# A fetch of list entries waits for the scatters of its own batch's units only

## The chip, the cores and the metric

The kernel runs on one core of one Trainium2 chip. The metric is the device time of one execution in microseconds (us), from a median over repeated runs. One core has five engines with instruction streams of their own: PE (TensorE, matrix products; PEld is its loading of weights), DVE (VectorE), ACT (ScalarE), POOL (GpSimd) and SP (SyncE, which here only reads registers and issues transfers). Engines wait for each other, and for transfers, on semaphores. Sixteen DMA engines carry the transfers of the core. An instruction that waits holds up what stands behind it in the stream of its own engine; this goes for the issue of a transfer too.

## The reference, cut to what matters

```
# gated linear attention, 4 batches x 8 heads x 768 steps x 48
for t in range(S):
    state = alpha[:, :, t, :, None] * state + einsum('bhd,bhe->bhde', k[:, :, t], v[:, :, t])
    y[:, :, t] = einsum('bhd,bhde->bhe', q[:, :, t], state)
x = y.transpose(0, 2, 1, 3).reshape(3072, 384)
# noisy top-2 router over 8 experts, each 384 -> 1024 -> 384
noisy = x @ w_gate + log1p(exp(x @ w_noise)) * noise
top2 = the two largest of noisy;  top2_w = softmax over them
for e in range(8):
    for k in range(2):
        mask = top2[:, k] == e
        h = maximum(x[mask] @ w1[e], 0)
        out[mask] += top2_w[mask, k, None] * (h @ w2[e])
```

All is float32. Each of the 3072 tokens is worked on by two experts, so there are 6144 pairs of token and expert.

## The kernel before, in words

**Attention.** The 3072 tokens are 24 chunks of 128, n = 0 to 23. The chunk of number n is loaded by four transfers on SP's queue (`load_values` L162, `load_chunk` L158: tiles `vt`, `a_in`, `k_in`, `q_in`, 192 KB each), two chunks at a time in buffers. A chunk's results go to the DRAM tensor `x_rows`, and its router decides two experts for each token.

**Lists.** Three chunks make a unit, u = 0 to 7. When a unit is routed, `give` (with `enter`, L585) ranks its 768 pairs within their experts and scatters one entry per pair (token, weight, expert, rank; 16 bytes) into the DRAM tensor `table`, where each expert has a region of its own. That is six indirect DMAs of 128 rows each, issued by POOL one after another (`put_entries`, L136). It happens at the end of chunk 3u+4.

**Tiles and batches.** The experts' work is cut into tiles of 128 entries of one expert. After each unit `plan_tiles` decides how many tiles the entries so far fill, and hands out a batch of them: `GIVEN = [0, 5, 11, 17, 23, 29, 35, 55]` gives where each unit's batch ends, so tiles 0 to 4 are given out after unit 1, 5 to 10 after unit 2, and so on to 29 to 34 after unit 6; the rest, up to 50 in the plain case, after unit 7. `plan` holds each tile's expert and first row in `table`. A batch of unit u is worked on beside chunks 3u+8 to 3u+10, so the work for one batch lies over the routing of later units.

**One tile.** It needs its 128 entries (`load_tab`, L687: a transfer `tab<-table` on SP's queue), the first-layer weights of its expert (`load_w1`, L695: `w<-in_moe_w_dram`, 1.5 MB, also on SP's queue, two buffers), its rows of x (`gather_x`, L719, an indirect DMA by POOL) and their transposes (`turn_x`, L728 on PE, L730 on DVE). `layer1` is L739 on PE with the ReLU by ACT at L741, in two halves; `layer2` is L751, with its scaling by ACT at L768. `get_half` (L758) fetches the other half of an output row; `combine` scatters by L769 and L776.

**Order.** The whole program is one order, written out by hand (L864 to L920). Pieces of a chunk and steps of tiles take turns; each engine works through its own instructions in that order. The tile numbered i has four steps, of which the first loads the weights for tile i+1 and gathers the rows for tile i+2. The first four fetches of a batch are issued together, two chunks ahead of the batch (L906). The later ones, the fifth and sixth, are put ahead of the first step of the tile four places earlier (L831):

```
if i + 4 < min(GIVEN[u], ALWAYS):
    steps[0] = lambda go=steps[0]: (load_tab(i + 4), go())
```

So on SP's queue the fetch for tile i+4 stands directly ahead of the weights for tile i+1. Each fetch is made to wait for all scatters into `table` that stand ahead of it in the order (`take_tile`, L144). When the first of the late fetches of a batch comes, the next unit's six scatters already stand ahead of it.

The list `entries` has the clearing of the table first, and then the scatters in order, 6 a unit.

Of the kernel before, what the change touches and what calls it, by code (L numbers as in the profile page):

```python
# [9 lines left out]
F32 = mybir.dt.float32  # L10
# [4 lines left out]
AFTER = mybir.DependencyInfo(mybir.DependencyClass.Sync, mybir.DependencyReason.DATA)  # L15
# [3 lines left out]
def kernel(  # L19
# [28 lines left out]
    nc = tc.nc  # L48
# [3 lines left out]
    C = 128  # L52
# [7 lines left out]
    UT = UC * C  # L60
    NU = NT // UC
# [13 lines left out]
    def pool(name, bufs, on=ctx, **kw):  # L75
        return on.enter_context(tc.tile_pool(name=name, bufs=bufs, **kw))
# [45 lines left out]
    table = dram.tile([TROWS, 4], U32, name="table")  # L122


    entries, taken = [], []

    def clear_table(on):
# [13 lines left out]
        tc.add_manual_dep(put.ins, entries[0].name, AFTER, reason="the table is cleared first")  # L141
        entries.append(put.ins)

    def take_tile(get):  # L144
        for put in entries:
            tc.add_manual_dep(get.ins, put.name, AFTER, reason="reads any row of the table")
        taken.append(get.ins)

    NIN = 2
# [526 lines left out]
    def experts(on):  # L676
# [7 lines left out]
        tabs, w1s, xts, os_, wheres = {}, {}, {}, {}, {}  # L684
        to_half, from_half, to_out = [], [], []

        def load_tab(i):  # L687
            if i >= NTILE:
                return
            r = nc.values_load(plan[0:1, i, 1:2], engines=[mybir.EngineType.SP], min_val=0, max_val=TROWS - C,  # L690
                               skip_runtime_bounds_check_because=WHY)
            tabs[i] = on["tab"].tile([C, 4], F32, name="tab")
            take_tile(nc.sync.dma_start(out=tabs[i], in_=table.bitcast(F32)[ds(r, C), :]))

        def load_w1(i):  # L695
            if i >= NTILE:
# [88 lines left out]
    def tile_steps(i, do, units):  # L785
        load_tab, load_w1, gather_x, turn_x, layer1, layer2, get_half, combine = do

        def first():
            if i + 1 < units[1]:
                load_w1(i + 1)  # L790
            if i + 2 < units[1]:
                gather_x(i + 2, units[0])
            layer1(i, 0)

        def second():
            layer1(i, 1)

        def third():
            if i + 1 < units[1]:
                turn_x(i + 1)  # L800
            get_half(i, units[0])
            layer2(i, 0)

        def fourth():
            layer2(i, 1)
            combine(i, units[0])

        return [first, second, third, fourth]

    def pools(es, name):  # L810
        on = {"one": pool(name + "one", 1, es), "two": pool(name + "two", 2, es), "three": pool(name + "three", 3, es),
              "tab": pool(name + "tab", 10, es)}
        for x, bufs in (("h", 2), ("o", 1), ("tp", 2), ("sc", 1), ("y", 1)):
            on[x] = pool(name + "ps_" + x, bufs, es, space=PS)
        return on


    with ExitStack() as es:
        on = pools(es, "")
        (load, load_v, alphas, keys, queries, scores, masked, turn_k, state, output, turn_y, route,  # L820
         choose_part, give, out_of_range) = fast_gla(on)
        do = experts(on)
        load_tab, load_w1, gather_x, turn_x = do[:4]
        starts = [0] + GIVEN[:-1]
        unit_of = [u for u in range(NU) for _ in range(starts[u], GIVEN[u])]

        def steps_of(i):
            u = unit_of[i]
            steps = tile_steps(i, do, (u + 1, min(GIVEN[u], ALWAYS)))
            if i + 4 < min(GIVEN[u], ALWAYS):  # L830
                steps[0] = lambda go=steps[0]: (load_tab(i + 4), go())  # L831
            return steps


        def last_tiles(i):
            if i == NTILE:
                return
            number = nc.values_load(tiles_i[0:1, 0:1], min_val=0, max_val=NTILE,
                                    skip_runtime_bounds_check_because="a count of tiles")
            with tc.If(number > i):  # L840
                load_tab(i)
                load_w1(i)
                gather_x(i, NU)
                turn_x(i)
                for step in tile_steps(i, do, (NU, i + 1)):
                    step()
                last_tiles(i + 1)


        LAG = 8  # L850
        held = []
        W2_AT = [0, 3, 6, 9, 12, 15, 18, 21, 24, 28, 32]
        beside = []
        for n in range(NT + 2 * UC):
            u, part = divmod(n - LAG, UC)
            beside.append([])
            if 0 <= u < NU - 1 and GIVEN[u] > starts[u]:
                each = -(-(GIVEN[u] - starts[u]) // UC)
                beside[n] = list(range(starts[u] + each * part, min(starts[u] + each * (part + 1), GIVEN[u])))
        while not beside[-1]:  # L860
            beside.pop()
        beside.append(list(range(starts[NU - 1], ALWAYS)))

        with tc.manual_schedule():  # L864
            load(0)
            load(1)
            load_v(0)
            for n in range(2):
                alphas(n)
                keys(n)  # L870
                queries(n)
                load(n + 2) if n == 0 else load_v(1)
            scores(0)
            masked(0)
            turn_k(0)
            for n, tiles in enumerate(beside):
                work = [step for i in tiles for step in steps_of(i)]
                chunk = [lambda: (load_v(n + 2), load(n + 3), state(n)), lambda: alphas(n + 2), lambda: keys(n + 2),
                         lambda: scores(n + 1), lambda: (queries(n + 2), masked(n + 1)),
                         lambda: (choose_part(n - 2, 1), route(n - 1)), lambda: turn_k(n + 1), lambda: output(n),  # L880
                         lambda: turn_y(n - 1)]
                last = [lambda: (choose_part(n - 1, 0), give(n - 2))]
                if n == 0:
                    last.append(lambda: held.append(load_router(on)))
                if n == 1:
                    last.append(lambda: clear_table(on["two"]))
                if n == 2:
                    chunk.insert(1, lambda: turn_noise(held.pop(), on))
                w2_parts = [lambda i=i: load_w2(i) for i in range(W2_AT[n], W2_AT[n + 1])] if n < len(W2_AT) - 1 else []

                if n < LAG:
                    last += w2_parts
                else:
                    chunk[0:0] = w2_parts
                if n == NT + 1:
                    chunk.insert(0, lambda: out_of_range(0))
                    last.append(lambda: out_of_range(1))

                for ahead in (2, 1):
                    nxt = beside[n + ahead] if n + ahead < len(beside) else []  # L900
                    if not nxt or nxt[0] not in starts:
                        continue
                    lo, u = nxt[0], unit_of[nxt[0]]
                    some = range(lo, min(lo + 4, GIVEN[u]))
                    if ahead == 2:
                        last.append(lambda some=some: [load_tab(i) for i in some])  # L906
                    else:
                        chunk.insert(3, lambda: (load_w1(lo), [gather_x(i, u + 1) for i in some[:2]]))
                        chunk.append(lambda: turn_x(lo))
                chunk += last  # L910
                done = 0
                for j in range(len(work)):
                    work[j]()
                    upto_j = len(chunk) * (j + 1) // len(work)
                    for piece in chunk[done:upto_j]:
                        piece()
                    done = upto_j
                for piece in chunk[done:]:
                    piece()
            last_tiles(ALWAYS)  # L920
    redo = nc.values_load(again_i[0:1, 0:1], min_val=0, max_val=2 * C,
                          skip_runtime_bounds_check_because="a count of at most 2 C rows")
    with tc.If(redo > 0):
        taken.clear()
        with ExitStack() as es:
            on = pool("g_clear", 1, es)
            clear_table(on)
        with ExitStack() as es:
            general_gla(es)
        with ExitStack() as es:  # L930
            do = experts(pools(es, "g_"))
            for i in range(4):
                do[0](i)
            do[1](0)
            for i in range(2):
                do[2](i, NU)
            do[3](0)
            for i in range(NTILE):
                do[0](i + 4)
                for step in tile_steps(i, do, (NU, NTILE)):  # L940
                    step()

# [29 lines left out]
```

## Time and profile before

| | |
|---|---|
| runs | median of 3: 877.54 us (875.82 to 878.76) |
| the profiled execution | 869.29 us, its span from first to last instruction 867.6 us |
| mean granted clock of PE in it | 0.944 of full speed |
| busy | PE 779.7 us (90%), POOL 339.1 (39%), DVE 274.5 (32%), ACT 198.8 (23%) |
| DMA | 146.59 MB moved, mean 169 GB/s |

The profile is one execution on the chip. Busy time is summed per engine over its span; idle time of an engine is put down to the last event that released it (an instruction of another engine, a DMA, "issue" where nothing is seen, "remote" where the event's origin isn't resolved). A row of the timeline is the start, the duration, the engine (SPq is SP's queue), the line of the kernel, the operation and what it writes and reads, and in square brackets how long the engine was idle before it and what ended that.

### The profile page before, as it was taken

What the parts mean: (1) busy time and instruction counts of PE and PEld (TensorE: products, weight loads), DVE (VectorE), ACT (ScalarE), POOL (GpSimd) and SP (SyncE); (2) the same over time, 40 slices, a digit from 0 to 9 for tenths busy, and PEclk for the clock granted to TensorE, in tenths of its full rate; (3) what the DMA queues carried; (4) which work ended last, traced back from release to release, by engine and by line L of the source; (5) the groups of instructions that cost most, each with busy time, mean ns of one, the idle gap of its engine ahead of it and who ended that gap; (6) DMA issues with size and microseconds to landing.
All of it is one profiled execution on the core that took longest, in us unless ns stands there. A gap on an engine that the chain in (4) does not pass through costs nothing. (4 is left out here: it accounts for less than half of the span.)

```text
span 867.6 us, 14567 instructions
## 1 busy us (share of the span) xinstructions
PE 779.7 (90%) x5249; PEld 636.5 (73%) x5249; DVE 274.5 (32%) x968; ACT 198.8 (23%) x383; POOL 339.1 (39%) x436
## 2 busy tenths in 40 slices
PE   7888788899899997999899995999599999999992
PEld 5777677688678775888678784787487788888881
DVE  7565755334433334125333241124111111111110
ACT  3343440224122321223122220122111111111110
POOL 4235435343625235334524344245333333333331
PEclk9898877999989999999989998999799999999997
DMA  9898784955295715974184515551555445555530
GB/s 175 190 271 212 216 181 140 270 172 141 57 276 161 223 61 126 256 201 135 35 277 142 195 67 176 186 192 53 177 183 199 163 167 175 190 193 195 201 115 13
DMA packets 158888, 146.59 MB, mean 169 GB/s; under 512 B 117612, under 2 KB 133698, under 8 KB 158804
## 3 DMA queue, kind: packets, MB, share of 16 engines
q1 hardware_dynamic: 136288, 111.79, 44.8%
q0 software_dynamic: 14592, 23.75, 9.4%
q10 hardware_dynamic: 7924, 9.97, 3.4%
q8 instruction: 47, 0.77, 0.4%
q14 instruction: 37, 0.30, 0.1%
HBM read 131.95 MB, written 30.00 MB: 187 GB/s over the span
## 5 line engine op out<-in xcount | busy, mean ns | idle before, releaser
L739 PE MATMUL h_ps<-xt,w 128*128 128x128 f32 x2448 | 293.3, 279 | 17.6 <-DMA w<-in_moe_w_dram 16.1
L739 PEld LDWEIGHTS h_ps<-xt,w 128*128 128x128 f32 x2448 | 286.8, 195 | 26.5 <-issue 16.8
L751 PE MATMUL o_ps<-w,h 128*128 x816 | 284.7, 498 | 3.6 <-issue 2.5
L751 PEld LDWEIGHTS o_ps<-w,h 128*128 128x128 f32 x816 | 152.7, 195 | 99.0 <-issue 11.7
L769 POOL DMA_INDIRECT half_rows<-o,where x51 | 61.2, 1200 | 303.5 <-ACT o L768 257.0
L741 ACT ACTIVATE h<-h_ps 128x512 f32<-128x512 f32 x102 | 60.9, 597 | 308.1 <-PE h_ps L739 168.6
L775 DVE TENSOR_TENSOR prev<-prev,o 128x384 f32<-128x384 f32 x51 | 28.5, 559 | 258.0 <-ACT o L768 233.6
L730 DVE COPY xt<-x_ps 128x384 f32<-128x384 f32 x51 | 28.1, 552 | 176.1 <-PE x_ps L728 164.8
L768 ACT ACTIVATE o<-o_ps,tab 128x384 f32<-128x384 f32 x51 | 29.6, 581 | 188.5 <-PE o_ps L751 188.5
L758 POOL DMA_INDIRECT prev<-half_rows,where x51 | 53.7, 1052 | 28.0 <-DMA half_rows<-o,where 13.6
L719 POOL DMA_INDIRECT x_in<-x_rows,where x51 | 53.5, 1049 | 24.1 <-issue 11.7
L776 POOL DMA_INDIRECT out_dram<-prev,where x51 | 51.1, 1002 | 17.9 <-issue 12.7
L136 POOL DMA_INDIRECT table<-entry,place_u x48 | 48.8, 1017 | 15.0 <-issue 12.2
L291 POOL TENSOR_TENSOR k_P<-k_P,over 128x512 f32<-128x512 f32 x24 | 28.3, 1180 | 65.5 <-DVE over L281 50.9
L275 DVE TENSOR_TENSOR_SCAN P_all<-a_all,least 128x516 f32<-128x516 f32 x24 | 30.7, 1280 | 55.3 <-ACT a_all L271 45.4
L345 POOL TENSOR_TENSOR S<-S,end 128x384 f32<-128x384 f32 x20 | 20.1, 1006 | 50.2 <-DVE S L343 49.4
L196 PE MATMUL y<-q_P,S 128*128 128x128 f32 x192 | 31.2, 315 | 3.7 <-ACT lgs L221 3.7
L263 PE MATMUL tp<-ident,k_in 128*128 128x128 f32 x96 | 17.7, 316 | 17.5 <-ACT tp L272 12.4
L314 PEld LDWEIGHTS sc<-q_P,k_P 48*128 48x128 f32 x384 | 26.1, 207 | 9.8 <-issue 6.6
L314 PE MATMUL sc<-q_P,k_P 48*128 48x128 f32 x384 | 31.0, 307 | 2.4 <-POOL k_P L291 2.4
L196 PEld LDWEIGHTS y<-q_P,S 128*128 128x128 f32 x192 | 28.6, 226 | 5.7 <-ACT lgs L221 4.3
L319 DVE COPY_PREDICATED MT<-upto,sc 128x512 f32<-128x512 uint32 x48 | 31.9, 718 | 0.0
(144 smaller groups left out, 667.5 us busy)
## 6 DMA issues: line engine op xcount, KB each, us to landing
w<-in_moe_w_dram SPq DMA_DIRECT2D x51, 1536.0 KB
w<-in_moe_w_dram SPq DMA_DIRECT2D x32, 384.0 KB
a_in<-in_alpha_dram SPq DMA_DIRECT2D x24, 192.0 KB
k_in<-in_k_dram SPq DMA_DIRECT2D x24, 192.0 KB
q_in<-in_q_dram SPq DMA_DIRECT2D x24, 192.0 KB
vt<-in_v_dram SPq DMA_DIRECT2D x24, 192.0 KB
x_rows<-y_sb ACTq DMA_DIRECT2D x24, 192.0 KB
half_rows<-y_sb ACTq DMA_DIRECT2D x24, 192.0 KB
```

The costliest lines, as they stand in the source:

```text
L136: put = nc.gpsimd.indirect_dma_start(out=table, out_offset=bass.IndirectOffsetOnAxis(ap=place, axis=0), in_=entry, in_offset=None, bounds_ ...
L196: nc.tensor.matmul(y[:, j, :], S_old[:, j].rearrange("p i d -> p (i d)"), q[:, j, :], start=j == 0, stop=False, skip_group_check=True)
L275: nc.vector.tensor_tensor_scan(P_all[:, 0:NP * CB], a_all[:, 0:NP * CB], least.rearrange("p j t -> p (j t)"), 0.0, op0=ALU.mult, op1=ALU.max)
L314: nc.tensor.matmul(c["sc"][i][:, j, :], c["k"][r, j, :], c["q"][r, j, :], start=True, stop=True)
L319: nc.vector.copy_predicated(MTs[n % 2][:, i], mask_upto, sc)
L719: nc.gpsimd.indirect_dma_start(out=x_in[i % NB], out_offset=None, in_=x_rows[0:units * UT, :], in_offset=bass.IndirectOffsetOnAxis(ap=wher ...
L739: nc.tensor.matmul(h_ps[:, fo, :], w1[:, a, ds((part * FO // 2 + fo) * C, C)], xt[:, a, :], start=a == 0, stop=a == KO - 1)
L741: nc.scalar.activation(os_[i]["h"][part], h_ps, AF.Relu)
L751: nc.tensor.matmul(o["ps"], o["h"][part][:, f, :], w2[:, ds(o["e"], 1), fo, :].rearrange("p o d -> p (o d)"), start=fo == 0, stop=fo == FO ...
L758: get = nc.gpsimd.indirect_dma_start(out=prev[i % 2], out_offset=None, in_=half_rows[0:units * UT, :], in_offset=bass.IndirectOffsetOnAxis ...
L769: put = nc.gpsimd.indirect_dma_start(out=half_rows[0:units * UT, :], out_offset=bass.IndirectOffsetOnAxis(ap=where[:, 1:2], axis=0), in_=o ...
L776: put = nc.gpsimd.indirect_dma_start(out=out, out_offset=bass.IndirectOffsetOnAxis(ap=where[:, 2:3], axis=0), in_=prev[i % 2], in_offset=N ...
```

## The change

`take_tile` is told how many units the batch of the tile was given out from. It keeps the waits for the clearing and for the scatters of these units (`2 * UT // C` = 6 a unit), and declares that there is no dependence on the later scatters. `load_tab` gets the number of units as an argument: `u + 1` for the batches in the hand-written order, `NU` = 8 (all units) for the tiles behind number 50 and for the general path that is entered only when a region overflows.

```diff
-    def take_tile(get):
-        for put in entries:
-            tc.add_manual_dep(get.ins, put.name, AFTER, reason="reads any row of the table")
+    def take_tile(get, units):
+        count = 1 + 2 * UT // C * units
+        for put in entries[:count]:
+            tc.add_manual_dep(get.ins, put.name, AFTER, reason="reads any row of the table that these fill")
+        for put in entries[count:]:
+            tc.declare_no_dep(get.ins, put, reason="rows behind those of the tile")
         taken.append(get.ins)
...
-        def load_tab(i):
+        def load_tab(i, units):
             if i >= NTILE:
                 return
...
-            take_tile(nc.sync.dma_start(out=tabs[i], in_=table.bitcast(F32)[ds(r, C), :]))
+            take_tile(nc.sync.dma_start(out=tabs[i], in_=table.bitcast(F32)[ds(r, C), :]), units)
...
-                steps[0] = lambda go=steps[0]: (load_tab(i + 4), go())
+                steps[0] = lambda go=steps[0]: (load_tab(i + 4, u + 1), go())
...
-                load_tab(i)
+                load_tab(i, NU)
...
-                        last.append(lambda some=some: [load_tab(i) for i in some])
+                        last.append(lambda some=some, u=u: [load_tab(i, u + 1) for i in some])
...
-                do[0](i)
+                do[0](i, NU)
...
-                do[0](i + 4)
+                do[0](i + 4, NU)
```

No instruction is added, removed or put elsewhere on any engine; lines behind the new ones move by four. What changes is what some fetches wait for. In the rows below a line is an instruction with its line, operation, what it writes and reads, and the semaphores that it waits for: DMASW are those of indirect DMAs issued by POOL, DMAHW those of other transfers, and DVE_, Activation_ and PE_ those of the engines (DVE, ACT, PE).

The first place is SP's queue in the batch of tiles 23 to 28, where the fetch for tile 27 (the first `tab` row) stands between the weights of tile 23 (`w_4702`) and those of tile 24 (`w_4932`). Before:

```order
L701 DMA w_4702<-in_moe_w_dram 128x3x1024 [waits DMAHW2_49,PE_49]
L690 TENSOR_LOAD plan
L693 ISA
L693 DMA tab<-table 128x4 [waits DMASW5_49,DMASW4_49,DMASW6_49,DMASW3_49,DMASW7_49,DMASW2_49,DMAHW5_49,DVE_49,Activation_49]
L698 TENSOR_LOAD plan
L701 ISA
L701 DMA w_4932<-in_moe_w_dram 128x3x1024 [waits DMAHW7_49,DMAHW6_49,PE_49]
L690 TENSOR_LOAD plan
L693 ISA
L693 DMA tab<-table 128x4 [waits Activation_49]
```

And after the change, the same place:

```order
L705 DMA w_4702<-in_moe_w_dram 128x3x1024 [waits DMAHW2_49,PE_49]
L694 TENSOR_LOAD plan
L697 ISA
L697 DMA tab<-table 128x4 [waits DMAHW3_49,DVE_49,Activation_49]
L702 TENSOR_LOAD plan
L705 ISA
L705 DMA w_4932<-in_moe_w_dram 128x3x1024 [waits DMAHW7_49,DMAHW4_49,PE_49]
L694 TENSOR_LOAD plan
L697 ISA
L697 DMA tab<-table 128x4 [waits DMAHW5_49,DMAHW1_49,Activation_49]
```

The fetch for tile 27 no longer waits for six semaphores of scatters, which were those of unit 6; the weights for tile 24 stand directly behind it as before. The DMAHW numbers, which are given out in turn, fall differently in a few rows: the weights for tile 24 wait on number 4 in place of 6, and the fetch for tile 28 (the last row) on two numbers more. The same goes for the first late fetch of each of the six batches that have one (tiles 4, 9, 15, 21, 27 and 33).

The second place is again SP's queue, earlier: the first of the four fetches issued together ahead of that batch (tile 23, the first `tab` row). Before:

```order
L701 DMA w_4492<-in_moe_w_dram 128x3x1024 [waits DMAHW5_49,DMAHW2_49,PE_49]
L690 TENSOR_LOAD plan [waits DVE_49]
L693 ISA
L693 DMA tab<-table 128x4 [waits DMAHW3_49,DVE_49,Activation_49]
L690 TENSOR_LOAD plan
L693 ISA
L693 DMA tab<-table 128x4 [waits DMAHW4_49,Activation_49]
```

After the change:

```order
L705 DMA w_4492<-in_moe_w_dram 128x3x1024 [waits DMAHW5_49,DMAHW2_49,PE_49]
L694 TENSOR_LOAD plan [waits DVE_49]
L697 ISA
L697 DMA tab<-table 128x4 [waits DMASW5_49,DMASW4_49,DMASW6_49,DMASW1_49,DMASW7_49,DMASW0_49,DMAHW3_49,DVE_49,Activation_49]
L694 TENSOR_LOAD plan
L697 ISA
L697 DMA tab<-table 128x4 [waits DMAHW4_49,Activation_49]
```

The six waits for scatters that the fetch of tile 21 had in the batch before (those for unit 5) stand at this fetch now. In all, seven fetches wait for scatters before, and seven after.

## Rows read from the trace of the kernel before

**Rows 1.** The page's first part: span, and PE's busy time and instructions.

```profile
span 867.6 us, 14567 instructions
PE 779.7 (90%) x5249; PEld 636.5 (73%) x5249; DVE 274.5 (32%) x968; ACT 198.8 (23%) x383; POOL 339.1 (39%) x436
```

**Rows 2.** Waits of PE: who waited for whom, us in all, times, longest us.

```profile
PE h_ps L739 <- DMA w<-in_moe_w_dram: 16.1, 3, 8.9
PE tp L263 <- ACT tp L272: 16.0, 7, 4.8
```

**Rows 3.** Waits of SP's queue, in the same columns.

```profile
SPq L693 <- DMA table<-entry,place_u: 129.1, 7, 37.6
```

**Rows 4.** Timeline of SP's queue, pieces of three stretches between 104 and 640 us.

```profile
105.29 3.09 SPq L158 DMA_DIRECT2D k_in<-in_k_dram  x1
...
153.75 0.00 SPq L693 DMA_DIRECT2D tab<-table  x1
...
492.95 0.38 SPq L701 DMA_DIRECT2D w<-in_moe_w_dram  x1
528.19 0.71 SPq L693 DMA_DIRECT2D tab<-table  x1
529.09 0.37 SPq L701 DMA_DIRECT2D w<-in_moe_w_dram  x1
...
558.38 3.32 SPq L693 DMA_DIRECT2D tab<-table  x4
...
612.77 0.37 SPq L701 DMA_DIRECT2D w<-in_moe_w_dram  x1
```

**Rows 5.** Timeline of PE in the batch of tiles 23 to 28, and at 156 us.

```profile
155.69 0.66 PE L263 MATMUL tp<-ident,k_in 128*128 128x128 f32 x4 [2.80 <-ACT tp L272]
...
503.03 2.92 PE L739 MATMUL h_ps<-xt,w 128*128 128x128 f32 x24
...
526.77 2.85 PE L751 MATMUL o_ps<-w,h 128*128 x8 [2.52 <-issue]
536.01 4.32 PE L739 MATMUL h_ps<-xt,w 128*128 128x128 f32 x24 [6.39 <-DMA w<-in_moe_w_dram]
```

**Rows 6.** Timeline of PE in the batch of tiles 29 to 34.

```profile
585.64 5.52 PE L739 MATMUL h_ps<-xt,w 128*128 128x128 f32 x48
...
608.56 2.85 PE L751 MATMUL o_ps<-w,h 128*128 x8 [1.12 <-ACT h L741]
620.32 7.49 PE L739 MATMUL h_ps<-xt,w 128*128 128x128 f32 x48 [8.91 <-DMA w<-in_moe_w_dram]
```

**Rows 7.** Timeline of DVE, the copies that take xt out of PSUM.

```profile
527.56 0.56 DVE L730 COPY xt<-x_ps 128x384 f32<-128x384 f32 x1 [6.16 <-remote]
...
610.69 0.56 DVE L730 COPY xt<-x_ps 128x384 f32<-128x384 f32 x1 [5.14 <-remote]
```

**Rows 8.** Timeline of POOL, scatters of unit 1 and the first and last of unit 6.

```profile
106.41 1.51 POOL L136 DMA_INDIRECT table<-entry,place_u  x1 [0.30 <-issue]
...
517.58 1.01 POOL L136 DMA_INDIRECT table<-entry,place_u  x1 [0.16 <-POOL entry L596]
...
524.01 0.97 POOL L136 DMA_INDIRECT table<-entry,place_u  x1 [0.31 <-issue]
```

**Rows 9.** Timeline of ACT, where it goes on during the scatters of units 1 and 6.

```profile
109.93 0.17 ACT L221 COPY lgs<-lg 128x16 f32<-128x16 f32 x1 [5.86 <-remote]
...
526.12 0.60 ACT L741 ACTIVATE h<-h_ps 128x512 f32<-128x512 f32 x1 [6.83 <-remote]
```

**Rows 10.** Windows: stretch, length, busy time of each engine (count), PEclk, DMA share, GB/s.

```profile
104.00:110.00 6.00, 1.95 (x16) 1.48 (x14) 5.76 (x16) 0.14 (x3) 5.07 (x5) 0.91 0.87 145
...
506.00:517.00 11.00, 9.85 (x64) 7.22 (x63) 2.85 (x13) 2.24 (x4) 2.15 (x2) 1.00 0.10 36
517.00:531.00 14.00, 10.10 (x58) 7.28 (x57) 4.52 (x28) 1.78 (x3) 9.39 (x13) 1.00 0.20 44
...
614.00:650.00 36.00, 29.68 (x187) 25.34 (x188) 4.45 (x23) 4.15 (x7) 11.50 (x12) 0.86 0.58 208
```

## The prediction

> **What bounds the kernel now.** I read the page's first part, then the waits of PE, the waits of SP's queue, and last the timelines of both at the places where they meet. PE is busy 779.7 of 867.6 us, 90% [rows 1], so its stream sets the end, and a change is worth what it takes out of that stream's gaps. Two causes top the list of its gaps: 16.1 us in three waits for a tile's first-layer weights, and 16.0 us in seven waits for the factor `tp` that ACT writes [rows 2]. SP's queue in its turn waited 129.1 us for scatters into `table`, at seven fetches, up to 37.6 us at one [rows 3]. That sum looks like the prize, and it is not: SP computes nothing, and its waiting costs only where something that stands behind the fetch is late for PE.
>
> It is late in two batches of the six. SP's queue issued a load of weights at 492.95 us, then nothing until 528.19, when the fetch for tile 27 went, and 0.9 us behind it, at 529.09, the weights for tile 24 [rows 4]. PE was done with the tile ahead at 526.77 + 2.85 = 529.62, and idled 6.39 us until it began tile 24 at 536.01 [rows 5]. The same in the next batch: the weights for tile 30 were issued at 612.77 [rows 4], PE was through at 608.56 + 2.85 = 611.41, and began at 620.32, 8.91 us later [rows 6]. The third wait is what is left: 16.1 - 6.39 - 8.91 = 0.8 us. In the other batches the fetch is held as long, but the weights behind it come in time, since beside chunks of attention PE has other work between two tiles.
>
> **What the change removes.** The first late fetch of each of six batches loses its wait for the unit routed meanwhile. The weights behind it are then free to go as soon as their buffer is. For tile 24 this buffer is the one that tile 22 read last; its second half ran from 503.03 for 2.92 us, to 505.95 [rows 5]. From issue to PE's start the weights took 536.01 - 529.09 = 6.9 us [rows 4, 5] and for tile 30 620.32 - 612.77 = 7.6 us [rows 4, 6]. So the weights of tile 24 are there by some 506 + 7 = 513 us, 16 us before PE is ready for them. For tile 30 the buffer comes free when tile 28 is through, 585.64 + 5.52 = 591.16 [rows 6]; the weights are there by 599, 12 us early. Both waits go whole, and the third, 0.8 us long, too: 16.1 us.
>
> *What is late next* at these two places decides whether the whole of it comes back. Tile 24 needs its transposed rows as well. DVE copied them out at 527.56 for 0.56 us, ending at 528.12, and for tile 30 at 610.69, ending at 611.25 [rows 7]. PE is through at 529.62 and 611.41: both copies are in time, the second by 0.16 us only. No gap is left behind.
>
> *The clock.* After both gaps PE's products take longer for a while: the 24 after the first 4.32 us where 24 took 2.92 before [rows 5], 1.4 us more; the 48 after the second 7.49 against 5.52 [rows 6], 2.0 us more. The granted clock was 1.00 up to 531 us and 0.86 in the 36 us from 614 [rows 10], so it fell in the gaps. [...] The gaps of 2.52 and 1.12 us shortly ahead [rows 5, 6] stay; were the clock to fall for these alone, the 3.4 would stay lost. In the stretch with the first of these it did not.
>
> **What it adds.** The first fetch of the next batch now has the waits for scatters. For tile 29, say, that is the first of four fetches issued from 558.38 us [rows 4]. The last scatter of unit 6 ended on POOL at 524.01 + 0.97 = 524.98 [rows 8], and the fetch that waited for its landing went at 528.19 [rows 4], 3.2 us later. So this wait is over 30 us before the instruction comes, and there are seven fetches with such waits as before. The waits on numbers of other transfers that fall anew (the two more at the fetch for tile 28) are for fetches of earlier tiles, issued a batch or more before. I take 0. The bound above is those 3.2 us at each of six fetches, were one to come while the scatters land; 19 us on a queue that has tens of us to spare ahead of a batch.
>
> **The sum.** 16.1 + 3.4 = 19.5 us. From the profiled execution's 869.29 us that gives 849.8. This execution lies 8.25 us (0.9%) under the median of the runs, 877.54, and outside their range; on the scale of the median the forecast is 877.54 - 19.5 = 858.0 us, 2.2% faster. A time within 0.3% (2.6 us) of the median is about what a measurement here can't tell from no change.
>
> **The rivals.**
>
> *More comes back.* At the scatters of each unit, ACT and DVE go on late: at 526.12 after 6.83 us in which nothing that the profile resolves released it, DVE at 527.56 after 6.16 [rows 7, 9]. PE's waits for `tp` are the trace of that on its side (2.80 us at 155.69 [rows 5], the others up to 4.8), and with them the 2.52 us and the 1.12. In all 16.0 + 2.5 + 1.1 = 19.6 us [rows 2, 5, 6]. These gaps lie in the very stretches in which SP is held by a fetch: SP went on at 153.75 [rows 4], 1.9 us before PE did. If SP's held wait causes them, they go, and the time is 858 - 19.6 = 838 us. Against it: during the scatters of unit 1 SP was not held, it issued chunk loads (at 105.29 [rows 4], beside a scatter at 106.41 [rows 8]), and ACT went on just as late, after 5.86 us [rows 9]. What is common to all is POOL issuing six scatters back to back (517.58 to 524.98 [rows 8]), and that stays. Chance 0.08.
>
> *Half comes back.* The next late thing takes one of the two places: the copy for tile 30 has 0.16 us in hand [rows 6, 7], and earlier traffic can move it. Then only the other place is won: 6.4 + 1.4 = 7.8 or 8.9 + 2.0 = 10.9 us, some 868 us. Chance 0.13.
>
> *Nothing comes back.* Another thing holds SP in the same stretch, such as the weights' buffer or a semaphore shared with a late transfer, and the weights come as late as before: 877.5. In the order only the waits named stand there, and the last of them, for the buffer, is over at 506 us. Chance 0.07.
>
> *Slower.* The weights, and in the early batches the chunk loads behind them, now move while POOL scatters. Before, the DMA engines were nearly empty then: a share of 0.20 in the scatters of unit 6 [rows 10], with SP held. If the scatters take longer for the company, the late goings-on of ACT and DVE grow, and PE's gaps with them, at each of six units. The price is at most the time of one load of weights, 7.6 us each, 46 us in all; it decides from 19.5 / 6 = 3.3 us a unit. In the extreme the time would be 877.5 - 19.5 + 46 = 904. Against it: the weights for tile 24 would move in 506 to 517 us, where the share was 0.10 [rows 10], and be there before the first scatter at 517.58 [rows 8]; and with a share of 0.87 at the scatters of unit 1, ACT's idling was 5.86 us, no longer than the 6.83 us at 0.20 [rows 9, 10]. A scatter did take 1.51 us there against 0.97 [rows 8], so a fraction of a us a unit is to be expected, inside the range. Chance 0.06.
>
> [...]
>
> **How the numbers follow.** Forecast 0.66, own range 851 to 865 (the clock's 3.4 us won or not, a us or two a unit lost to the company, and as much for the change of clock from run to run). More 0.08, half 0.13, nothing 0.07, slower 0.06. The range of 8 in 10 reaches over the half case on one side and into the first rival's on the other: 842 to 870 us. Faster 0.66 + 0.08 + 0.13 = 0.87, same 0.07, slower 0.06.
>
> **What would show it.** In the profile of the changed kernel PE's waits for weights should be gone from the list, or under 1 us. SP's waits for the table should fall from 129.1 us to a few. The weights for tile 24 and tile 30 should be issued at about 23 and 21 us before PE begins that tile, and the 24 and 48 products should take 2.9 and 5.5 us. PE's waits for `tp` should be as long as before, 16 us within 3. If those have gone, the first rival is right; if they have grown beyond 35 us, the last one. I'd be wrong above all if PE's 6.39 and 8.91 us come back under another name at the same place, xt or h.

## The result and the profile after

The changed kernel took 819.73 us (median of 4 runs, 812.12 to 822.61) where before took 876.68 us (4 runs, 868.33 to 878.76) beside it: a ratio of 0.9354, 95% interval 0.9266 to 0.9441. That is 57 us, about three times the 19.5 us of the forecast, and below its range. The profiled execution took 819.84 us, its span 818.1.

The waits of PE after the change, the longest three groups (who waited for whom, us in all, times, longest):

```profile
PE tp L267 <- DMA a_in<-in_alpha_dram: 9.7, 3, 5.2
PE total L627 <- DVE picked L595: 5.8, 7, 1.2
PE tp L267 <- ACT tp L276: 3.9, 4, 1.7
```

The wait for weights of [rows 2] is gone, as forecast. But the wait for ACT's `tp` has gone from 16.0 to 3.9 us as well, which I had said would stay. On SP's queue no fetch waits for scatters any more, where [rows 3] had 129.1 us; its timeline at the places of [rows 4] is:

```profile
479.54 0.37 SPq L705 DMA_DIRECT2D w<-in_moe_w_dram  x1
480.48 0.35 SPq L697 DMA_DIRECT2D tab<-table  x1
...
554.33 0.37 SPq L705 DMA_DIRECT2D w<-in_moe_w_dram  x1
```

These are the weights for tiles 24 and 30. PE begins those tiles at 500.23 and 572.99, with nothing to wait for and at a granted clock of 1.00:

```profile
500.23 2.84 PE L743 MATMUL h_ps<-xt,w 128*128 128x128 f32 x24
...
567.83 5.33 PE L755 MATMUL o_ps<-w,h 128*128 x16
572.99 5.52 PE L743 MATMUL h_ps<-xt,w 128*128 128x128 f32 x48
```

The weights are issued 20.7 and 18.7 us ahead, and the 24 and 48 products take 2.84 and 5.52 us where [rows 5, 6] had 4.32 and 7.49. The gaps of 2.52 and 1.12 us ahead of the second half of `o_ps` [rows 5, 6] are gone too: all 16 products run in one piece. ACT tells why. In the scatters of unit 6, where it idled 6.83 us [rows 9], it now goes on as soon as PE is through, the second time 0.04 us after PE's products ended at 489.30 + 5.60 = 494.90:

```profile
492.26 0.60 ACT L745 ACTIVATE h<-h_ps 128x512 f32<-128x512 f32 x1 [4.43 <-PE h_ps L743]
494.94 0.60 ACT L745 ACTIVATE h<-h_ps 128x512 f32<-128x512 f32 x1 [2.08 <-PE h_ps L743]
```

I call what is gone the lags: in six units, while POOL issues its six scatters, ACT had gone on 3.4 to 6.1 us after PE's last product for it, and in the last two of them DVE's copy of xt 5.9 and 5.8 us after. (The expectations below speak of 3 to 9 us; 9.05 us is ACT's longest idle time before it goes on, of which 6.1 us lie behind PE's product.) Laid over each other, product by product, the two profiles part in steps at the six batches that have a late fetch, 48 us in all by the last product. At first sight that is my first rival, the one in which the held fetch makes the lags. The experiments say otherwise.

### The profile page after: what moved, and what is told of

It reads as the page before. It is cut to its first block, busy times and chain, and to the rows that moved or that the text cites. A ratio compares the mean times of both kernels' runs of the same rounds, so it can differ in the third digit from the quotient of the medians.

```text
span 818.1 us, 14568 instructions
## 1 busy us (share of the span) xinstructions
PE 768.1 (94%) x5249; PEld 630.7 (77%) x5249; DVE 273.6 (33%) x968; ACT 198.8 (24%) x383; POOL 339.5 (41%) x436
## 5 line engine op out<-in xcount | busy, mean ns | idle before, releaser
L743 PE MATMUL h_ps<-xt,w 128*128 128x128 f32 x2448 | 289.3, 277 | 1.4 <-DVE xt L734 1.4
L743 PEld LDWEIGHTS h_ps<-xt,w 128*128 128x128 f32 x2448 | 283.4, 193 | 9.2 <-DVE xt L734 1.6
L755 PE MATMUL o_ps<-w,h 128*128 x816 | 277.1, 488 | 0.0
L755 PEld LDWEIGHTS o_ps<-w,h 128*128 128x128 f32 x816 | 149.2, 190 | 91.5 <-issue 2.3
L137 POOL DMA_INDIRECT table<-entry,place_u x48 | 51.0, 1063 | 15.0 <-issue 10.7
L318 PEld LDWEIGHTS sc<-q_P,k_P 48*128 48x128 f32 x384 | 26.1, 207 | 10.5 <-issue 5.9
L285 DVE TENSOR_TENSOR_SCAN over<-a_all,P_all 128x515 f32<-128x515 f32 x24 | 30.2, 1259 | 0.8
```

The costliest lines, as they stand in the source:

```text
L137: put = nc.gpsimd.indirect_dma_start(out=table, out_offset=bass.IndirectOffsetOnAxis(ap=place, axis=0), in_=entry, in_offset=None, bounds_ ...
L318: nc.tensor.matmul(c["sc"][i][:, j, :], c["k"][r, j, :], c["q"][r, j, :], start=True, stop=True)
L743: nc.tensor.matmul(h_ps[:, fo, :], w1[:, a, ds((part * FO // 2 + fo) * C, C)], xt[:, a, :], start=a == 0, stop=a == KO - 1)
L755: nc.tensor.matmul(o["ps"], o["h"][part][:, f, :], w2[:, ds(o["e"], 1), fo, :].rearrange("p o d -> p (o d)"), start=fo == 0, stop=fo == FO ...
```

## The experiments

Kernels that are told together ran on one chip, with before beside them. Not all ran on the same chip, and this turned out to matter, so they are told by chip. Each chip was used at one time only, so a chip and its state at that time can't be told apart; I say chip for both. The letters H, P and so on are names of theories, which the expectations explain.

**First chip (lags): four kernels.** The first is before, unchanged.

> The kernel before, unchanged, once more. In the profile of before ACT and DVE go on 3 to 9 us late after PE's last product at all scatters of units 2 to 7, 2.8 us late at those of unit 1, and about 1 us late in the last tiles (694 to 826 us), where no fetch is held; after the change all of these lags are gone. Theory H (a fetch held on SP's queue makes the lags): here the six lags of 3 to 9 us are there again. Theory P (the lags belong to this execution or to the loaded program as a whole, not to the held fetch): if to the execution, they may be gone and the time about 835 to 850 us; if to the program, they are there again, those of 1 us in the last tiles too.

876.06 us in one run. The lags are there: ACT's wait with no resolved releaser is 46.4 us in 6 times, after 43.5 in the first profile.

The second keeps all waits and changes the order on SP's queue:

```diff
-                steps[0] = lambda go=steps[0]: (load_tab(i + 4), go())
+                steps[0] = lambda go=steps[0]: (go(), load_tab(i + 4))
```

> All waits of before are kept; only the late fetch stands behind the weights of the next tile on SP's queue and no longer ahead of them. It leaves the fetch held as long as before. My forecast's two terms (16.1 us of waits for weights and 3.4 us of slow products) should come back alone: about 858 us, with the six lags still there under theory H. Theory P: the lags are there or gone whatever SP does; if gone, about 830 us, with SP's queue still waiting some 100 us for the table.

852.12 us against 872.47, ratio 0.9771 (0.9701 to 0.9842): 20.4 us, the forecast's 19.5 within the interval. The lags stay. Of its waits, those of SP's queue at the table:

```profile
SPq L693 <- DMA table<-entry,place_u: 115.3, 10, 22.7
```

And those of ACT at the ReLU, with no releaser that the profile resolves ("remote"):

```profile
ACT h L741 <- remote: 47.0, 6, 9.0
```

The queue is held for 115.3 us still, and PE's waits for weights are gone. So here a fetch is held at no cost to PE, as the weights are not behind it.

The third has the change in the first four batches alone:

```diff
-                steps[0] = lambda go=steps[0]: (load_tab(i + 4, u + 1), go())
+                steps[0] = lambda go=steps[0]: (load_tab(i + 4, u + 1 if u < 5 else NU), go())
...
-                        last.append(lambda some=some, u=u: [load_tab(i, u + 1) for i in some])
+                        last.append(lambda some=some, u=u: [load_tab(i, u + 1 if u < 5 else NU) for i in some])
```

> The change in the batches of units 1 to 4 alone (tiles 4, 9, 15 and 21); the fetches of tiles 27 and 33 wait as before. By the products' starts of the two profiles, 26 of the 48 us were won by the end of the fourth batch. Theory H: these 26 us alone, with the lags of the first four batches gone and those of 4.8 and 3.4 us, and the waits of 6.4 and 8.9 us, still there: about 845 us. Theory P: the lags are gone everywhere or there everywhere; if gone, only the two waits of 15 us and their slow products remain against the changed kernel: about 840 us, with no lag at the scatters of units 6 and 7; if there, about 875 us.

871.67 us, ratio 0.9984 (0.9952 to 1.0017): nothing. ACT's unresolved wait, 45.3 us in 6 times, is as in before (43.5 in 6), though in four batches no fetch is held. This fells theory H: the held fetch does not make the lags. (Under theory H this kernel would have taken about 845 us.)

The fourth makes another program out of before, with no wait changed:

```diff
+    idle = const.tile([C, 4], F32, name="idle")
+    nc.gpsimd.memset(idle, 0.0)
```

> The kernel before with one tiny fill on POOL's engine at its start that nothing reads, so that the program is another one while no wait changes. Theory H: as before, 877 us, with all lags. Theory P, if the lags hang on how the program lies in memory: they may go, 840 to 850 us.

871.56 us, ratio 1.0001 (0.9965 to 1.0036), with the lags (ACT's unresolved wait 43.9 us in 6 times): that small a change of the program doesn't remove them.

**Second chip (lags): four kernels.** The changed kernel again; with the same fill; with the change in the batches of units 5 and 6 alone (the condition of the third kernel turned round, `u > 4`); and with the fetch behind the weights as well.

> The changed kernel once more. So far the late goings-on are in all five profiles of four programs (before twice, swap, early, null), everywhere in the run, and in none of the changed kernel. Theory C (they were absent by the chip or the session in which the changed kernel ran): here they are there, about 845 to 850 us. Theory G (they hang on the program): none again, 812 to 823 us.

> The changed kernel with one tiny fill on POOL's engine that nothing reads. Theory G1 (the program's waits decide: none of its fetches waits for a scatter of a unit that is still under way): no lags, about 820 us. Theory G2 (how the program happens to lie in memory decides): the lags may be back, about 848 us.

> The change in the batches of units 5 and 6 alone (tiles 27 and 33); the first four batches wait as before. My forecast's two terms come back, 19 us, in any theory: at most about 858 us. Theory G1: as four fetches are still held, the lags are there through the whole run: 855 to 860 us. Theory G2: there or gone; if gone, about 830 us.

> The changed kernel with the late fetch behind the weights on SP's queue, as in swap, and without the waits. Theory G1: no lags, about 820 us as the changed kernel. Theory G2: there or gone; if there, about 848 us, like swap.

Measured: 862.84 us (one run), 856.13 (ratio 0.9841, 0.9805 to 0.9877), 855.62 (0.9846, 0.9805 to 0.9887) and 856.14 (0.9829, 0.9778 to 0.9879), against 869.10 of before. All four have the lags: ACT's unresolved wait at the ReLU is 54.1, 46.6, 47.0 and 46.4 us. Two things follow. The changed kernel gains 13.0 us here with the fill and 6.3 in the one run without it, where the forecast had 19.5; the expectations had 845 to 850 us with lags. Its lags are as those of before; in its first profile the same program had none, so theory G falls. And the two late batches alone bring all of it, 13.5 us, as the first four brought nothing on the other chip.

The kernel with the fill tells where a part of the rest of the 19.5 us may have gone. The gaps ahead of the second half of `o_ps` in the two late batches, 2.52 and 1.12 us in [rows 5, 6], are longer there:

```profile
PE o_ps L757 <- issue: 3.9, 1, 3.9
PE o_ps L757 <- ACT h L747: 3.0, 1, 3.0
```

That would be 6.9 - 3.6 = 3.3 us lost again, and 19.5 - 3.3 = 16.2, which the interval of its ratio (10.7 to 16.9 us) holds. It is argued, not shown: before was not profiled on this chip, and in its second profile, on the first chip, these gaps were 3.2 and 2.5 us long already.

**Third chip (no lags): two kernels.** The changed kernel timed again, and one in which the six scatters of a unit are issued one at a time between the pieces of the next chunk:

```diff
-                put_entries(place_u[:, k, c:c + 1], entry.bitcast(U32)[:, c, k, :])
+                puts.append(lambda c=c, k=k: put_entries(place_u[:, k, c:c + 1], entry.bitcast(U32)[:, c, k, :]))
+        while puts and not spread[0]:
+            puts.pop(0)()
...
+                spread[0], done = True, 0
+                chunk = [lambda go=go: (go(), [puts.pop(0)() for _ in puts[:1]]) for go in chunk]
```

> The changed kernel a third time, now timed against before on one chip. In the first session it took 812 to 823 us with no late goings-on; in the second, in one run, 862.84 us with all of them. Theory S (the lags are there or not by the chip and the loading of the program, for the changed kernel as for others, and the change itself is worth my 19.5 us): either about 852 us, that is 19 to 20 below before, with the lags, or about 820 us without them, and then before on the same chip should have lost them too. Theory R (the changed kernel alone can be free of them): about 820 us while before stays at 868 to 878 us.

> The changed kernel with the six scatters of a unit issued one at a time between the pieces of the next chunk, no longer back to back. If back-to-back indirect DMAs by POOL make ACT and DVE go on late (three to nine us after six of them, two after five, one after four), the lags at the bursts go and 20 to 28 us with them where the changed kernel shows lags: about 828 us; where it shows none, no difference. If a lag belongs to each scatter by itself, 1 us each, nothing is won: 850 to 856 us.

819.72 us (ratio 0.9356, 0.9315 to 0.9398) and 819.45 (0.9360, 0.9311 to 0.9409) against 877.29 of before. Going by these times, both within 0.3 us of the 819.73 of the first result, neither had the lags. So the first result stands, and the second chip's stands too. What before looks like on such a chip was still not known; my theories had taken it that it has the lags.

**Fourth chip (no lags): four kernels together.**

> The kernel before, profiled on the same chip as the next three. Theory K (a chip, or its state, gives the lags to every kernel or to none): lags here exactly if the changed kernel next to it has them; without lags about 840 us by my count. Theory R (only the changed kernel can be free of them): lags here, 870 to 880 us, whatever the changed kernel does.

> The changed kernel beside it. 812 to 824 us without lags, or 850 to 863 us with them. Under theory R it is free of them on some chips, under K together with before.

> All waits kept, the late fetch behind the weights. With lags 19 to 20 us below before, as in the first run of this kernel. On a chip where the changed kernel shows no lags: under theory K none here, and about 825 us; under theory R, if the held fetch is what brings them there, they are here too and the time is 20 us below before.

> The change in the first four batches alone. With lags everywhere, no gain, as in its first run. On a chip where the changed kernel shows none: under theory K none here, and 20 us above the changed kernel; under theory R with a held fetch as the cause, lags at the scatters of units 6 and 7 alone, none at the others, and about 30 us below before.

Measured: before 884.68 us (883.27 in 7 runs beside it), changed 819.61, swap 820.36 (ratio 0.9297, 0.9263 to 0.9330), early 847.95 (0.9595, 0.9554 to 0.9636). No lags in any of them (ACT has no unresolved wait in their profiles): theory K holds, and theory R falls. But before without lags is not at 840 us, as K had it; it is slower than with them. Its waits of PE show where its time goes:

```profile
PE h_ps L739 <- DMA w<-in_moe_w_dram: 50.0, 6, 10.5
PE tp L263 <- DMA a_in<-in_alpha_dram: 5.8, 1, 5.8
...
PE tp L263 <- ACT tp L272: 4.7, 5, 1.5
```

Six waits for weights, one in each batch with a late fetch, 50.0 us, in place of three and 16.1 [rows 2]. The six rows of PE's timeline in which they end:

```profile
164.29 4.52 PE L739 MATMUL h_ps<-xt,w 128*128 128x128 f32 x24 [5.27 <-DMA w<-in_moe_w_dram]
...
251.25 5.37 PE L739 MATMUL h_ps<-xt,w 128*128 128x128 f32 x24 [7.40 <-DMA w<-in_moe_w_dram]
...
351.88 4.59 PE L739 MATMUL h_ps<-xt,w 128*128 128x128 f32 x24 [8.79 <-DMA w<-in_moe_w_dram]
...
452.16 5.49 PE L739 MATMUL h_ps<-xt,w 128*128 128x128 f32 x24 [7.90 <-DMA w<-in_moe_w_dram]
...
549.08 4.95 PE L739 MATMUL h_ps<-xt,w 128*128 128x128 f32 x24 [10.11 <-DMA w<-in_moe_w_dram]
...
634.26 7.70 PE L739 MATMUL h_ps<-xt,w 128*128 128x128 f32 x48 [10.54 <-DMA w<-in_moe_w_dram]
```

PE's products in them are slow. In before's first profile the granted clock was 0.66 and 0.74 over the two rows behind such a wait, of 4.32 and 7.49 us, and 1.00 over those of 2.92 and 5.52 [rows 5, 6]; on the fourth chip its mean over the execution was 0.933 in before and 0.966 in the changed kernel. Against the 2.92 us of 24 and the 5.52 of 48 the six rows take 1.6, 2.5, 1.7, 2.6, 2.0 and 2.2 us more, 12.5 in all. 50.0 + 12.5 = 62.5 us; 883.27 - 819.61 is 63.7. That is the difference to within 1.2 us, by the forecast's own two terms. The change in four batches leaves the last two waits:

```profile
PE h_ps L743 <- DMA w<-in_moe_w_dram: 22.7, 2, 11.9
```

Its median lies 28.3 us above the changed kernel, where theory K had 20: 22.7 us, and 3.8 of slow products behind them (4.72 and 7.48 us in place of 2.92 and 5.52). These are from its longest run, 853.40 us, the one that was profiled. And swap, with every wait kept, gets everything, 820.36 us, though its queue is held for 137.5 us in all, as its waits of SP's queue show:

```profile
SPq L693 <- DMA table<-entry,place_u: 137.5, 11, 23.4
```

**Fifth and sixth chip (no lags).** The spread scatters were to show whether back-to-back scatters make the lags, which needed a chip that has them.

> The changed kernel beside the spread one. So far chips came in two kinds: on two of them (two sessions) ACT and DVE go on 3 to 9 us late at the scatters in every kernel, on three sessions in none. On the first kind 855 to 863 us, on the second 815 to 824.

> The changed kernel with the six scatters of a unit one at a time between the pieces of the next chunk. On a chip of the second kind the same as the changed kernel, as in its first run. On one of the first kind: if back-to-back indirect DMAs make the lags there, the lags of 3 to 9 us go and the time falls from about 857 to 830 us; if each indirect DMA does by itself, they are spread out and the time stays within 5 us.

> The kernel before once more, to tell the kind of chip: with lags at the scatters (865 to 878 us, under 20 us of waits for weights) or without (877 to 885 us, about 50 us of waits for weights in six batches).

> The changed kernel with scatters spread over a chunk. On a chip without lags 816 to 824 us. On one with lags: if back-to-back indirect DMAs make them, about 830 us and no lag over 2 us; if each indirect DMA does, 852 to 860 us.

821.91 us (ratio 0.9323, 0.9276 to 0.9369) and 823.51 (0.9300, 0.9243 to 0.9358) against 882.84 on the fifth; before 887.39 and spread 822.83, one run each, on the sixth. Going by these times neither chip had the lags, and on the sixth PE waited for ACT's `tp` 5.0 and 5.8 us, where it is 14.9 to 21.5 on the chips with lags; so that question was not answered. Before had 51.4 us of waits for weights on the sixth, in six times: the fourth chip was no accident.

## Why the prediction was wrong

**What bounds the kernel** was right: PE's stream, and in it what stands behind a held fetch.

**What the change removes** was right in kind and wrong in size. The step that failed is the sentence that in the other batches the weights behind the fetch "come in time, since beside chunks of attention PE has other work between two tiles". That put these waits at nothing, and I gave no row for it. PE has the same work there with lags and without; it was the lag that moved this work behind the issue of the weights. The batch of tiles 5 to 10 shows it. In before, in the first profile, the timeline of SP's queue has the held fetch and the weights behind it:

```profile
238.76 0.23 SPq L693 DMA_DIRECT2D tab<-table  x1
239.59 0.37 SPq L701 DMA_DIRECT2D w<-in_moe_w_dram  x1
```

PE's timeline there, in the same profile, up to the products that need these weights:

```profile
240.15 1.11 PE L263 MATMUL tp<-ident,k_in 128*128 128x128 f32 x4 [4.82 <-ACT tp L272]
241.06 4.91 PE L751 MATMUL o_ps<-w,h 128*128 x8
245.90 1.16 PE L314 MATMUL sc<-q_P,k_P 48*128 48x128 f32 x16
...
247.49 2.84 PE L739 MATMUL h_ps<-xt,w 128*128 128x128 f32 x24
```

The same kernel on the fourth chip, first SP's queue:

```profile
242.77 0.35 SPq L693 DMA_DIRECT2D tab<-table  x1
243.72 0.37 SPq L701 DMA_DIRECT2D w<-in_moe_w_dram  x1
```

Then PE, up to the wait at 251.25 that is shown above:

```profile
239.00 0.60 PE L263 MATMUL tp<-ident,k_in 128*128 128x128 f32 x4
239.44 2.75 PE L751 MATMUL o_ps<-w,h 128*128 x8
242.11 1.16 PE L314 MATMUL sc<-q_P,k_P 48*128 48x128 f32 x16
243.20 0.66 PE L263 MATMUL tp<-ident,q_in 128*128 128x128 f32 x4
```

With lags PE idles 4.82 us for ACT, then runs eight products in 4.91 us, at a granted clock of 0.56, that take 2.75 on the other chip, and comes to the tile 247.49 - 239.59 = 7.9 us after the weights were issued: just when they land, going by the 6.9 and 7.6 us of the prediction. Without lags it is through at 243.20 + 0.66 = 243.86, 0.1 us after the issue, and idles 7.40 us. The lag cost 4.82 us of idling and 2.2 of slower products, about as much: one stall covered the other. On a chip with lags, dropping the wait of these batches leaves the lag where it is and wins nothing (early: 0.9984); only the two late batches, where the weights still came later, give anything (swap 20.4 us, late 13.5). On a chip without lags all six give. Rows are shown for one of the four covered batches; early speaks for the four together, with 0.9984 on a chip with lags and 0.9595 on one without.

**The sum.** Terms 16.1 and 3.4 us (the latter the 1.4 and 2.0 us of slow products) measured 50.0 and 12.5 us on the fourth chip. In the result the products of both places take 2.84 and 5.52 us at a granted clock of 1.00: there the 3.4 us were won. On the chips with lags 19.5 us was about right for swap (20.4, interval 13.8 to 26.1) and too much for the three kernels timed in four runs on the second chip (13.0 to 13.5), in part probably by the gaps ahead of `o_ps` that the forecast had left as they were. The profile that it was read from shows the lags, and the changed kernel's in the result doesn't. Of before's runs beside it no trace was taken: that they had no lags either is argued from the ratio, 0.9354, which the third chip gave again as 0.9356, and is not shown. The 57 us of the result itself are therefore taken apart only on the fourth chip.

**What is late next, the added waits:** in the result nothing took the freed places, and no fetch waits on SP's queue for a scatter after the change, so both costs of 0 held. On the second chip, with lags, the first of them probably didn't, as told there.

**The rivals.** "More comes back" named the time nearest to the result and the sign that came (`tp` waits gone), by a wrong mechanism: the lags do not hang on the held fetch, and before was no faster where they are absent (883.27 us on the fourth chip) than where they are present (872.47 and 869.10). That it came near in time is luck. "Half" and "nothing" did not come. "Slower" did not either. In the changed kernel the weights do move beside the scatters, with a DMA share of 0.57 in the window around those of unit 6 (0.20 before [rows 10]):

```profile
490.00:504.00 14.00, 14.00 (x97) 11.88 (x97) 5.07 (x30) 2.47 (x5) 10.44 (x13) 1.00 0.57 153
```

PE is busy for all of its 14.00 us there, at a granted clock of 1.00, and POOL's six scatters take 0.97 to 0.99 us each, where they took 0.97 to 1.01 before. PE paid nothing for the company here.

**The sign I passed by.** The profiled execution, 869.29 us, lay outside the three runs of before, 875.82 to 878.76. I scaled the sum by it and did not ask whether its trace showed the same waits as the runs had. On the chips with lags before had medians of 872.47 and 869.10 us, on those without 877.29, 883.27 and 882.84. It was a hint and no proof: on the first chip, with lags, runs of before reached 877.75 us.

**Open.** Why some chips show the lags and others don't. They came in every kernel on two chips and in the first profile, in no kernel on four chips and in the first run of the changed one; they are 6 or 7 unresolved waits of ACT at the ReLU each time, and the changed kernel and before each ran both with them and without. Whether it is the chip or its state at the time is open too. Whether back-to-back scatters are needed for them was not tried on a chip that has them.

## What to carry to other kernels

A pattern that stands in the program six times and costs in two of them is hidden in four: name the work that hides it, by a row, before these are put down at nothing. If what hides it is itself a stall of another kind, the two must be priced together, since here 7.0 us of lag (4.82 + 2.2) hid a wait of 7.40, which came forward where the lag was gone. And where the profiled execution's time lies outside the runs', its trace may be of another case than the one that is timed: work out the sum for both. In the code, a load that is needed soon does not belong behind a wait in one engine's queue; moving it ahead (swap) got all that dropping the wait did on the fourth chip, 820.36 against 819.61 us. On chips with lags the two were not timed side by side.

## What the hardware showed unexpectedly

The same program has a wait on some chips that it hasn't on others, and its total time hides it: before is not slower with the wait (872.47 us on the first chip, 883.27 on the fourth). In before's first profile ACT's ReLU at unit 3 began at 238.10, though PE's last product into its input ended at 229.12 + 2.87 = 231.99 us, as its timelines of PE and ACT have it:

```profile
229.12 2.87 PE L739 MATMUL h_ps<-xt,w 128*128 128x128 f32 x24
...
238.10 0.60 ACT L741 ACTIVATE h<-h_ps 128x512 f32<-128x512 f32 x1 [9.05 <-remote]
```

The changed kernel on the second chip had the same wait at the same place:

```profile
240.49 0.60 ACT L745 ACTIVATE h<-h_ps 128x512 f32<-128x512 f32 x1 [9.03 <-remote]
```

Before, on the fourth chip, had none:

```profile
232.94 2.87 PE L739 MATMUL h_ps<-xt,w 128*128 128x128 f32 x24
...
235.85 0.60 ACT L741 ACTIVATE h<-h_ps 128x512 f32<-128x512 f32 x1 [2.98 <-PE h_ps L739]
```

The last begins 0.04 us after PE's products ended (232.94 + 2.87 = 235.81 us). In the profile the lagging kind is known by the word "remote" in ACT's waits: 43.5 to 54.1 us of idle time in 6 or 7 times at the ReLU on chips with lags, none in the changed kernel's first profile and in the four on the fourth chip.

It is not ACT alone. In the changed kernel on the second chip the loads of weights on SP's queue, which wait for PE to be through with their buffer, have such waits too:

```profile
SPq L705 <- remote: 81.2, 6, 19.8
```

The changed kernel with the fill has 6 of them too (81.3 us), that with the fetch behind the weights 6 (82.8), the one with the change in four batches 4 (38.9, on the first chip) and the one with it in two batches 2 (36.0): as many as batches have no held fetch. On the fourth chip no kernel has them. What ACT, DVE and these loads wait for is PE. Why PE's end releases them late is not shown.
